# First product of the experts for the last 1,024 tokens: seven products of half blocks in place of eight

## Chip, cores and metric

One core of one Trainium2 chip. The time is the device time of one execution in microseconds (us); the kernel before has a median of 1032.53 us over 3 runs (1032.23 to 1032.94). TensorE is PE in the profile (PEld is its weight load), VectorE DVE, ScalarE ACT, GpSimd POOL; SP issues the DMAs.

## What is computed

Causal attention with a decay (4 batches, 8 heads, 576 tokens, head size 64), and on its output a mixture of 4 experts with two products each:

```python
attn_out = _attn_ref(**attn_kwargs)
x = attn_out.transpose(0, 2, 1, 3).reshape(B * S, H * D)   # 2304 x 512
p = domain_probs / (domain_probs.sum(-1, keepdims=True) + 1e-09)
for e in range(E):                                          # E = 4
    h = np.maximum(x @ w1[e], 0.0)                          # w1[e]: 512 x 1024
    out += p[:, e:e + 1] * (h @ w2[e])                      # w2[e]: 1024 x 512
```

All is in float32. TensorE is fed with float32r, so each product is made of three: a value is split into a high part (rounded to float32r) and a low part (the rest), and high x high, high x low and low x high are added in PSUM.

## The kernel before

**Tokens** are in 9 chunks of 256 (`CH`), numbered in the order in which the attention finishes them. **Hidden units** are in 32 blocks of 128, eight for each expert. A weight tile `wr` is 128 x 1024 (512 KB): its left half is w1 for one block (four slices of 128 columns, one for each quarter of the 512 inputs), its right half w2 for that block. `w_load` (line 579) issues its DMA on SP into one of 2 buffers, `w_split` (line 584) makes the high part `wh` on ACT and the low part `wl` with two subtractions of 512 columns on POOL (on DVE for the even ones of the first 16 tiles). `wh` and `wl` have 6 buffers each.

**A step** (class `Step`, line 604) is one chunk with two hidden blocks. `l1` (line 610) makes the hidden values: 2 blocks x 4 slices x 3 = 24 matmuls, 256 columns each, into a PSUM tile of `ps_1`. `gate` (line 628) applies the relu and splits: ACT writes `gh`, DVE writes `gl`. `l2` (line 641) is the second product: 2 halves of the chunk x 2 blocks x 3 = 12 matmuls of 512 columns into two tiles of `ps_2`, which two steps (`ps` 0 and 1) fill together. `gather` (line 660) then adds the tile, times the expert's probability, to the chunk's accumulator `acc` on DVE, and after the last one issues the output DMA.

**The order** is `SWEEPS` (line 24): sweep 0 has 28 steps with chunks 0 to 2, sweep 1 has 52 with chunks 1 to 4, sweep 2 has 64 with chunks 5 to 8 (each of 16 pairs of weight tiles meets the four chunks one after another). The main loop (line 797) writes `l1` of step n, then `l2` of step n - 1, and `w_split` for tiles 6 further on when a pair has met its last chunk. Instructions run on each engine in an order that a planner sets while the program is built: by the order written, but an instruction that is not ready in the planner's own model of time lets later ones go ahead.

**The attention** is cut into small pieces (`head_steps`, line 540), each with a cost: for a head of the second half of the tokens three pieces of scores (2072 in all), three of transposes (1500) and one of the product with v (600), so 4172. `pace` (line 727) writes these pieces between the steps, so that the summed cost follows a broken line through goals: a chunk must be done `LEAD` = 3 steps ahead of its first use. The pieces of the 24 heads that follow the startup in the first half and the 32 heads of the second half add up to 169,120. Its last instruction is `fin` (line 490), which writes the attention's output: for chunks 0 to 4 split into `xh` and `xl`, for chunks 5 to 8 as float32 into `xf`, and `widen` (line 527) splits these when the chunk is first used (ACT `xh`, DVE `xl`, 1024 columns each).

Of the kernel before, what the change touches and what calls it, by code (L numbers as in the profile page):

```python
# [8 lines left out]
F32 = mybir.dt.float32  # L9
# [8 lines left out]
CH = 256  # L18
# [5 lines left out]
SWEEPS = (  # L24
    ((0,), (0,), (0, 1), (0, 1, 2)),
    ((1, 2, 3, 4), (1, 2, 3, 4), (2, 3, 4), (3, 4)),
    ((5, 6, 7, 8), (5, 6, 7, 8), (5, 6, 7, 8), (5, 6, 7, 8)),
)
DIRECT = (0, 1, 2, 3, 4)
LEAD = 3  # L30
W_DVE = tuple(range(0, 16, 2))
W_SLOT = (4, 6)
NEAR = 2
JOBS = ((0, 0), (1, 0), (2, 0), (3, 0), (0, 1), (1, 1), (2, 1), (3, 1))
# [34 lines left out]
def fused(ctx: ExitStack, tc: tile.TileContext, qk, v, f, probs, w, out):  # L69
# [3 lines left out]
        tc.tile_pool(name=name, bufs=bufs, space=bass.MemoryType.PSUM)  # L73
    )
    const = SB("const", 1)
    raw_p = SB("raw", 1)
    hi_p = SB("hi", 2)
    p_p = SB("p", 6)
    pt_p = SB("pt", 1)
    v_p = SB("v", 2)  # L80
    x_p = SB("x", 2)
    st_p = SB("st", 4)
    xh_p = SB("xh", 4)
    xf_p = SB("xf", 4)
    w_p = SB("w", 6)
    wr_p = SB("wr", 2)
    g_p = SB("g", 2)
    acc_p = SB("acc", 4)
    dr_p = ctx.enter_context(tc.tile_pool(name="dr", bufs=4, space=bass.MemoryType.DRAM))
    ps_a = PS("ps_a", 4)  # L90
    ps_1 = PS("ps_1", 2)
# [432 lines left out]
                            op=ALU.mult,  # L524
                        )

    def widen(c):
        th, tl = x_tiles(c)
        nc.scalar.activation(out=th, in_=xf[c], func=AF.Copy)
        nc.vector.tensor_tensor(out=tl, in0=xf[c], in1=th.bitcast(F32), op=ALU.subtract)  # L530


    jobs = []
    for b, half in JOBS:
# [39 lines left out]


    wh, wl, wraw = {}, {}, {}
    NW = len(SWEEPS) * E * (FF // 128)

    def w_load(n):
        if n < NW and n not in wraw:  # L580
# [1 line left out]
            nc.sync.dma_start(out=wraw[n], in_=w[n % 32])  # L582

    def w_split(n):
        if n >= NW:
            return
        w_load(n)
        wh[n] = w_p.tile([128, 1024], F32R, tag="wh", name=f"wh{n}")
        wl[n] = w_p.tile([128, 1024], F32R, tag="wl", name=f"wl{n}")
        r = wraw.pop(n)  # L590
        nc.scalar.activation(out=wh[n], in_=r, func=AF.Copy)  # L591
        for a in (0, 512):
            z = a + 512
            eng = nc.vector if n in W_DVE else nc.gpsimd
            eng.tensor_tensor(  # L595
                out=wl[n][:, a:z], in0=r[:, a:z], in1=wh[n][:, a:z].bitcast(F32), op=ALU.subtract
            )
        w_load(n + 1)
        w_load(n + 2)

    acc = {}
    l2 = {}

    class Step:
# [36 lines left out]
        def l2(self, q):  # L641
            tt, fi = divmod(q, 2)
            if self.ps == 0 and fi == 0:
                l2[tt] = ps_2.tile([128, DM], F32, tag="l2", name=f"l2_{self.nm}_{tt}")
            n = self.w0 + fi
            a = self.gh[:, fi, tt * 128 : (tt + 1) * 128]
            z = self.gl[:, fi, tt * 128 : (tt + 1) * 128]
            x, y = wh[n][:, 512:], wl[n][:, 512:]
            for m, (lhsT, rhs) in enumerate(((a, x), (a, y), (z, x))):
                nc.tensor.matmul(  # L650
                    out=l2[tt],
                    lhsT=lhsT,
                    rhs=rhs,
                    start=(self.ps == 0 and fi == 0 and m == 0),
                    stop=(self.ps == 1 and fi == 1 and m == 2),
                )
            if self.ps == 1 and fi == 1:
                self.gather(tt)

        def gather(self, tt):  # L660
            c, e = self.c, self.g // 2
            if tt == 0:
                seen[c] += 1
            if c not in acc:
                acc[c] = acc_p.tile([128, 2, DM], F32, tag="acc", name=f"acc{c}")
            sc = prob[:, 2 * c + tt, e : e + 1]
            if seen[c] == 1:
                nc.vector.tensor_scalar(
                    out=acc[c][:, tt, :], in0=l2[tt], scalar1=sc, scalar2=None, op0=ALU.mult
                )  # L670
            else:
                nc.vector.scalar_tensor_tensor(  # L672
                    out=acc[c][:, tt, :],
                    in0=l2[tt],
                    scalar=sc,
                    in1=acc[c][:, tt, :],
                    op0=ALU.mult,
                    op1=ALU.add,
                )
            if seen[c] == 2 * E:  # L680
                for o, r0, n in rows_of(c, tt):
                    nc.sync.dma_start(out=out[r0 : r0 + n, :], in_=acc[c][o : o + n, tt, :])

    seen = {c: 0 for c in range(NCH)}
    steps = [
# [9 lines left out]
    for n in range(len(heads) + 1):  # L695
        if n >= FIRST:
            asteps.extend(head_steps(n))
        stage_end.append(len(asteps))
    cost = [0.0]
    for c, _ in asteps:  # L700
        cost.append(cost[-1] + c)
# [16 lines left out]
        first.setdefault(t.c, n)  # L718
    marks = [(0, cost[need[steps[0].c]])]
    goals = sorted((max(n - LEAD, 1), cost[need[c]]) for c, n in first.items() if n > 0)  # L720
    while goals:
        n0, c0 = marks[-1]
        best = max(goals, key=lambda m: ((m[1] - c0) / (m[0] - n0), m[0]))
# [73 lines left out]
    for n in range(len(steps) + 1):  # L797
        cur = steps[n] if n < len(steps) else None
        if cur is not None:
            if cur.c not in used:  # L800
                used.add(cur.c)
                upto(need[cur.c])
                if cur.c not in DIRECT:
                    widen(cur.c)
            for q in range(4):
                cur.l1(q)
                pace(n + q / 8)
            cur.gate()
        if prev is not None:
            for q in range(4):  # L810
                prev.l2(q)
                pace(n + (q + 4) / 8)
            if prev.c == SWEEPS[prev.s][prev.g // 2][-1]:
                base = prev.w0 + 6
                w_split(base)
                w_split(base + 1)
        prev = cur


# [41 lines left out]
```

## Time and profile before

| | |
|---|---|
| time of the profiled execution | 1032.68 us |
| its span, first to last instruction | 1031.0 us |
| median of 3 runs | 1032.53 us |
| PE busy | 1004.5 us, 97% |
| DVE, ACT, POOL busy | 541.7, 451.9, 320.3 us |
| mean granted TensorE clock | 0.988 of full speed |

Matmuls are pipelined: the record of one matmul (mean 285 ns for 256 columns) is longer than the distance to the next. What a matmul costs in a dense stretch is therefore read from the chain of work that ended last, which counts the matmuls of a stretch and its length. In the chain and in the timeline a line begins with its start and its duration in us; a bracket at the end of a timeline line tells how long the engine had been idle before and who released it. In a list of groups, "x144 | 99.3, 690 |" means 144 instructions, 99.3 us in all, 690 ns each, and behind the next bar is the idle time before them.

### The profile page before, as it was taken

How to read it: one execution, taken by the hardware profiler on the slowest of the kernel's cores; microseconds unless marked ns; L12 is line 12 of the kernel's file. 1: busy time of each engine (PE TensorE's matmuls, PEld its weight loads, DVE VectorE, ACT ScalarE, POOL GpSimd, SP SyncE). 2: the span in 40 equal slices, each digit the busy share in tenths (PEclk: the TensorE clock that was granted, in tenths of full speed). 3: DMA queues.
4: the chain of work that ended last, by engine and by line, in shares of the span. 5: the costliest groups of instructions: out<-in, count | busy, mean ns of one | idle time of the engine just before them, and what ended most of it. 6: DMA issues, size and time to landing. Idle time of an engine off the chain costs nothing.

```text
span 1031.0 us, 16823 instructions
## 1 busy us (share of the span) xinstructions
PE 1004.5 (97%) x6544; PEld 917.3 (89%) x6544; DVE 541.7 (53%) x1184; ACT 451.9 (44%) x909; POOL 320.3 (31%) x346
## 2 busy tenths in 40 slices
PE   4799999999999999999999999999999999999998
PEld 4697899989999999999999999999999999999997
DVE  6767766586877856677466665532222222222222
ACT  6766666566656535445455455422121211212110
POOL 4756876341403204031223144213030311303010
PEclk9599999999999999999999999999999999999999
DMA  5445544252412214032131331211120202112001
GB/s 179 134 148 166 164 133 130 74 165 85 131 50 90 90 50 131 15 93 95 62 118 54 111 118 62 90 54 47 37 82 1 83 21 62 51 32 82 1 22 62
DMA packets 30447, 87.02 MB, mean 84 GB/s; under 512 B 3268, under 2 KB 5376, under 8 KB 30368
## 3 DMA queue, kind: packets, MB, share of 16 engines
q1 hardware_dynamic: 30368, 85.94, 26.4%
q8 instruction: 52, 0.85, 0.3%
q14 instruction: 27, 0.22, 0.1%
HBM read 81.06 MB, written 4.87 MB: 83 GB/s over the span
## 4 chain that ended last, share of the span: by engine, by line
PE 89%; DMA 4%; DVE 3%; ACT 2%; issue 1%; POOL 1%; SPq 1%; ACTq 0%; POOLq 0%; DVEq 0%
PE l L620 38%; PE l L650 36%; PE s L314 5%; PE t L406 5%; PE o L456 4%; DMA wr<-in_w 2%; DVE v L249 1%; PE b L374 1%; DMA raw<-in_qk 1%; ACT wh L591 1%; DMA pr_r<-in_probs 1%; POOL wl L595 0%; DVE xl L506 0%; DVE p L328 0%; DVE wl L595 0%
## 5 line engine op out<-in xcount | busy, mean ns | idle before, releaser
L595 POOL TENSOR_TENSOR wl<-wr,wh 128x512 fp32r<-128x512 f32 x176 | 228.1, 1325 | 351.3 <-ACT wh L591 345.5
L620 PE MATMUL l<-xh,wh 128*128 128x256 f32 x1152 | 330.9, 288 | 1.2 <-ACT xh L503 1.0
L620 PE MATMUL l<-xl,wh 128*128 128x256 f32 x1152 | 328.8, 285 | 0.1
L620 PE MATMUL l<-xh,wl 128*128 128x256 f32 x1152 | 328.2, 285 | 0.0
L632 DVE SCALAR_TENSOR_TENSOR gl<-l,gh 128x512 fp32r<-128x512 f32 x144 | 99.3, 690 | 276.3 <-ACT gh L631 275.5
L650 PE MATMUL l<-wh,gh 128*128 128x512 f32 x576 | 230.5, 400 | 0.4 <-DVE rs L362 0.4
L650 PE MATMUL l<-wl,gh 128*128 128x512 f32 x576 | 227.8, 395 | 0.0
L620 PEld LDWEIGHTS l<-xh,wh 128*128 128x128 f32 x1152 | 220.9, 192 | 6.5 <-ACT xh L503 1.6
L620 PEld LDWEIGHTS l<-xl,wh 128*128 128x128 f32 x1152 | 221.3, 192 | 5.8 <-DVE xl L506 0.5
L650 PE MATMUL l<-wh,gl 128*128 128x512 f32 x576 | 225.8, 393 | 0.0
L620 PEld LDWEIGHTS l<-xh,wl 128*128 128x128 f32 x1152 | 221.3, 192 | 0.7 <-DVE wl L595 0.2
L631 ACT ACTIVATE gh<-l 128x512 fp32r<-128x512 f32 x144 | 85.6, 594 | 277.7 <-PE l L620 276.9
L343 ACT ACTIVATE p<-p,nm 128x576 f32<-128x576 f32 (+2 forms) x160 | 96.1, 601 | 97.3 <-DVE nm L328 96.7
L591 ACT ACTIVATE wh<-wr 128x1024 fp32r<-128x1024 f32 x96 | 99.9, 1054 | 69.3 <-DMA wr<-in_w 39.9
L650 PEld LDWEIGHTS l<-wh,gl 128*128 128x128 f32 x576 | 108.3, 188 | 22.6
L650 PEld LDWEIGHTS l<-wh,gh 128*128 128x128 f32 x576 | 108.8, 189 | 16.8 <-issue 0.6
L650 PEld LDWEIGHTS l<-wl,gh 128*128 128x128 f32 x576 | 109.0, 189 | 14.9
L672 DVE SCALAR_TENSOR_TENSOR acc<-l,prob,acc 128x512 f32<-128x512 f32 x126 | 94.0, 748 | 26.8 <-PE l L650 24.0
L328 DVE CUSTOM_DVE_ANT_0 p<-s,mask 128x288 f32<-128x288 f32 (+2 forms) x160 | 75.6, 477 | 49.4 <-PE s L314 48.4
L262 POOL CAST q<-raw 64x320 fp32r<-64x320 f32 (+1 forms) x56 | 27.1, 484 | 235.7 <-PE s L314 210.9
L423 DVE TENSOR_TENSOR ptl<-t,pth 128x320 fp32r<-128x320 f32 (+2 forms) x120 | 66.1, 553 | 60.9 <-ACT pth L416 60.4
L406 PE MATMUL t<-ident,p 128*128 128x128 f32 x480 | 83.7, 283 | 5.6 <-ACT p L343 3.5
(73 smaller groups left out, 1003.2 us busy)
## 6 DMA issues: line engine op xcount, KB each, us to landing
wr<-in_w SPq DMA_DIRECT2D x96, 512.0 KB
raw<-in_qk SPq DMA_DIRECT2D x16, 896.0 KB
raw<-in_qk SPq DMA_DIRECT2D x12, 512.0 KB
vr<-in_v SPq DMA_DIRECT2D x16, 320.0 KB
out<-acc SPq DMA_DIRECT2D x16, 256.0 KB
first<-in_qk SPq DMA_DIRECT2D x4, 512.0 KB
vr<-in_v SPq DMA_DIRECT2D x12, 128.0 KB
first<-in_v SPq DMA_DIRECT2D x1, 512.0 KB
```

The lines of the kernel that those rows point to most:

```text
L314: nc.tensor.matmul(out=ps[:, at : at + z - a], lhsT=lhsT, rhs=rhs, start=(m == 0), stop=(m == 1),)
L328: nc.vector.tensor_tensor_reduce(out=pt[:, a:z], in0=ps, in1=mask[:, m0 + a : m0 + z], scale=-0.125, scalar=BIG if n == 0 else nm[:, col : ...
L343: nc.scalar.activation(out=pt[:, :w_], in_=pt[:, :w_], func=AF.Exp, scale=-1.0, bias=self.nmax[hh][:, c : c + 1], accum_out=self.ssum[:, h ...
L406: nc.tensor.transpose(ps[:, at : at + 128], self.p[hh, it][:, TOK0[jt] : TOK0[jt] + 128], ident)
L423: nc.vector.tensor_tensor(out=lo[:, a0 + first : a0 + at - first], in0=ps[:, 2 * first : at], in1=hi[:, a0 + first : a0 + at - first].bitc ...
L591: nc.scalar.activation(out=wh[n], in_=r, func=AF.Copy)
L595: eng.tensor_tensor(out=wl[n][:, a:z], in0=r[:, a:z], in1=wh[n][:, a:z].bitcast(F32), op=ALU.subtract)
L620: nc.tensor.matmul(out=self.l1p[:, fi, :], lhsT=lhsT, rhs=rhs[:, k, :], start=(k == 0 and m == 0), stop=(k == 3 and m == 2),)
L631: nc.scalar.activation(out=self.gh, in_=self.l1p, func=AF.Relu)
L632: nc.vector.scalar_tensor_tensor(out=self.gl, in0=self.l1p, scalar=0.0, in1=self.gh.bitcast(F32), op0=ALU.max, op1=ALU.subtract,)
L650: nc.tensor.matmul(out=l2[tt], lhsT=lhsT, rhs=rhs, start=(self.ps == 0 and fi == 0 and m == 0), stop=(self.ps == 1 and fi == 1 and m == 2),)
L672: nc.vector.scalar_tensor_tensor(out=acc[c][:, tt, :], in0=l2[tt], scalar=sc, in1=acc[c][:, tt, :], op0=ALU.mult, op1=ALU.add,)
```

## The change

Sweep 2 goes. In its place come 16 pairs `Big(p)`, each one pair of weight tiles (256 hidden units) with all 1,024 tokens of chunks 5 to 8. The first product is seen as 2 x 2 blocks (hidden blocks of 128, inputs in halves of 256, tokens in halves of 512: chunks 5, 6 and chunks 7, 8) and made with seven products in place of eight (Strassen's scheme in Winograd's form): four sums of weight blocks (`SUMS`) and four of token blocks (`XSUMS`), seven products of 2 slices x 3 = 6 matmuls with 512 columns (`PRODUCTS`), and seven sums of the results (`Big.l1`). `x_piece` makes and splits the seven token blocks once, in two parts each; `big_split` makes and splits the weight blocks of a pair into three `wh` and `wl` tiles (the four sums; the three unsummed blocks; w2). The blocks of x lie in a pool that is opened in the memory of the attention's pools once those are closed (`open_late`); the split hidden values lie where `xh` and `xl` were. `gather` is called for each pair (16 times a chunk half) in place of each second step (8 times). `wr` gets a third buffer. The attention's pieces, with 14 of `x_piece` behind them (costs 200 and 300, 3,600 in all), have as last goal step 76 of the 80 steps that are left. A line of "..." marks what is left out.

```diff
 SWEEPS = (
     ((0,), (0,), (0, 1), (0, 1, 2)),
     ((1, 2, 3, 4), (1, 2, 3, 4), (2, 3, 4), (3, 4)),
-    ((5, 6, 7, 8), (5, 6, 7, 8), (5, 6, 7, 8), (5, 6, 7, 8)),
 )
 DIRECT = (0, 1, 2, 3, 4)
 LEAD = 3
 W_DVE = tuple(range(0, 16, 2))
+LAST = (5, 6, 7, 8)
+AHEAD = 4
...
     st_p = SB("st", 4)
-    xh_p = SB("xh", 4)
     xf_p = SB("xf", 4)
     w_p = SB("w", 6)
-    wr_p = SB("wr", 2)
+    wr_p = SB("wr", 3)
     g_p = SB("g", 2)
     acc_p = SB("acc", 4)
+    early = ExitStack()
+    chunks = ExitStack()
+    AT = lambda name, bufs: early.enter_context(tc.tile_pool(name=name, bufs=bufs))
+    raw_p = AT("raw", 1)
+    hi_p = AT("hi", 2)
+    p_p = AT("p", 6)
+    pt_p = AT("pt", 1)
+    v_p = AT("v", 2)
+    x_p = AT("x", 2)
+    xh_p = chunks.enter_context(tc.tile_pool(name="xh", bufs=4, side="right"))
...
-    def widen(c):
-        th, tl = x_tiles(c)
-        nc.scalar.activation(out=th, in_=xf[c], func=AF.Copy)
-        nc.vector.tensor_tensor(out=tl, in0=xf[c], in1=th.bitcast(F32), op=ALU.subtract)
-
...
     wh, wl, wraw = {}, {}, {}
-    NW = len(SWEEPS) * E * (FF // 128)
+    NW = 3 * E * (FF // 128)
+    NS = len(SWEEPS) * E * (FF // 128)
...
     def w_split(n):
-        if n >= NW:
+        if n >= NS:
+            if n % 2 == 0:
+                big_split((n - NS) // 2)
             return
...
         w_load(n + 1)
         w_load(n + 2)
+        w_load(n + 3)
...
                 )
             if self.ps == 1 and fi == 1:
-                self.gather(tt)
...
+                gather(self.c, tt, self.g // 2, l2[tt], 2 * E)
+    def gather(c, tt, e, ps, times):
...
+        if seen[c] == times:
+            for o, r0, n in rows_of(c, tt):
+                nc.sync.dma_start(out=out[r0 : r0 + n, :], in_=acc[c][o : o + n, tt, :])
...
+    SUMS = (
+        (1, (1, 0), (1, 1), ALU.add),
+        (2, 1, (0, 0), ALU.subtract),
+        (3, (0, 0), (1, 0), ALU.subtract),
+        (4, (0, 1), 2, ALU.subtract),
+    )
+    XSUMS = (
+        (1, (0, 1), (0, 0), ALU.subtract),
+        (2, (1, 1), 1, ALU.subtract),
+        (4, 2, (1, 0), ALU.subtract),
+        (3, (1, 1), (0, 1), ALU.subtract),
+    )
+    PRODUCTS = {
+        1: (1, 256, (0, 0)),
+        2: (1, 512, (1, 0)),
+        3: (0, 768, (1, 1)),
+        4: (1, 0, 4),
+        5: (0, 0, 1),
+        6: (0, 256, 2),
+        7: (0, 512, 3),
+    }
+    late = ExitStack()
+    rh, rl, bw, xs_ = {}, {}, {}, {}
+    def open_late():
+        early.close()
+        late.x = late.enter_context(tc.tile_pool(name="rx", bufs=1))
+    def x_piece(i, k, op=None, *of):
+        if k not in rh:
+            rh[k] = late.x.tile([128, 2, 512], F32R, tag=f"rh{k}", name=f"rh_{len(rh)}")
+            rl[k] = late.x.tile([128, 2, 512], F32R, tag=f"rl{k}", name=f"rl_{len(rl)}")
+        hi, lo = (t[:, :, CH * i : CH * (i + 1)] for t in (rh[k], rl[k]))
+        x_of = lambda b: (
+            xf[LAST[2 * b[1] + i]][:, 2 * b[0] : 2 * b[0] + 2, :]
+            if type(b) is tuple
+            else xs_[b, i]
+        )
+        if op is None:
+            x = x_of(k)
+        else:
+            x = xs_[k, i] = late.x.tile([128, 2, CH], F32, tag="t", name=f"rx{k}_{i}", bufs=2)
+            nc.gpsimd.tensor_tensor(out=x, in0=x_of(of[0]), in1=x_of(of[1]), op=op)
+        nc.scalar.activation(out=hi, in_=x, func=AF.Copy)
+        nc.vector.tensor_tensor(out=lo, in0=x, in1=hi.bitcast(F32), op=ALU.subtract)
+    def big_split(p):
+        if p >= 16:
+            return
+        n = NS + 2 * p
+        w_load(n)
+        w_load(n + 1)
+        r = [wraw.pop(n), wraw.pop(n + 1)]
+        part = lambda b: r[b[0]][:, 256 * b[1] : 256 * b[1] + 256]
+        t = late.x.tile([128, 4, 256], F32, tag="wt", name=f"wt{p}", bufs=1)
+        w_of = lambda b: part(b) if type(b) is tuple else t[:, b - 1, :]
+        for k, a, z, op in SUMS:
+            nc.gpsimd.tensor_tensor(out=t[:, k - 1, :], in0=w_of(a), in1=w_of(z), op=op)
+        tiles = []
+        for k in range(3):
+            tiles.append(
+                [
+                    w_p.tile([128, 1024], F32R, tag=x, name=f"b{x}{p}_{k}") for x in ("wh", "wl")
+                ]
+            )
+        f = t.rearrange("p k n -> p (k n)")
+        jobs_ = [
+            (0, 0, f),
+            (1, 0, part((1, 1))),
+            (1, 256, part((0, 0))),
+            (1, 512, part((0, 1))),
+            (2, 0, r[0][:, 512:]),
+            (2, 512, r[1][:, 512:]),
+        ]
+        for k, c, x in jobs_:
+            w_ = x.shape[1]
+            hi, lo = (y[:, c : c + w_] for y in tiles[k])
+            nc.scalar.activation(out=hi, in_=x, func=AF.Copy)
+            for a in range(0, w_, 512):
+                z = min(a + 512, w_)
+                nc.gpsimd.tensor_tensor(
+                    out=lo[:, a:z], in0=x[:, a:z], in1=hi[:, a:z].bitcast(F32), op=ALU.subtract
                 )
+        bw[p] = tiles
+        for k in range(2, 5):
+            w_load(n + k)
+    class Big:
+        def __init__(self, p):
+            self.p, self.e = p, p // 4
+        def product(self, m):
+            ps = ps_a.tile([128, 512], F32, tag="a", name=f"m{self.p}_{m}")
+            k0, c, b = PRODUCTS[m]
+            a, z = (t[:, c : c + 256] for t in bw[self.p][k0])
+            for k in range(2):
+                o = slice(128 * k, 128 * k + 128)
+                for i, (lhsT, rhs) in enumerate(((a, rh[b]), (a, rl[b]), (z, rh[b]))):
+                    nc.tensor.matmul(
+                        out=ps,
+                        lhsT=lhsT[:, o],
+                        rhs=rhs[:, k, :],
+                        start=(k == 0 and i == 0),
+                        stop=(k == 1 and i == 2),
+                    )
+            return ps
+        def add(self, tag, ps, x, op=ALU.add, out=None, flip=False):
+            if out is None:
+                out = g_p.tile([128, 512], F32, tag=tag, name=f"u{self.p}_{len(self.u)}")
+                self.u.append(out)
+            if x is None:
+                nc.scalar.activation(out=out, in_=ps, func=AF.Copy)
             else:
+                a, z = (x, ps) if flip else (ps, x)
+                nc.vector.tensor_tensor(out=out, in0=a, in1=z, op=op)
+            return out
+        def gate(self, b, x):
+            hi, lo = (
+                late.h.tile([128, 512], F32R, tag=t, name=f"{t}{self.p}_{b[0]}{b[1]}")
+                for t in ("hh", "hl")
+            )
+            nc.scalar.activation(out=hi, in_=x, func=AF.Relu)
+            nc.vector.scalar_tensor_tensor(
+                out=lo, in0=x, scalar=0.0, in1=hi.bitcast(F32), op0=ALU.max, op1=ALU.subtract
+            )
+            self.h[b] = hi, lo
+        def l1(self):
+            self.h, self.u = {}, []
+            e1 = self.add("gh", self.product(1), None)
+            u2 = self.add("gl", self.product(6), e1)
+            self.add(None, self.product(2), e1, out=e1)
+            self.gate((0, 0), e1)
+            p5 = self.product(5)
+            u4 = self.add("gh", p5, u2)
+            self.add(None, self.product(7), u2, out=u2)
+            c22 = self.add("gl", p5, u2)
+            self.gate((1, 1), c22)
+            self.add(None, self.product(3), u4, out=u4)
+            self.gate((0, 1), u4)
+            self.add(None, self.product(4), u2, ALU.subtract, out=u2, flip=True)
+            self.gate((1, 0), u2)
+        def l2(self, q):
+            for u in (2 * q, 2 * q + 1):
+                half, o = divmod(128 * u, 512)
+                pool, tag = ((ps_2, "l2"), (ps_1, "l1"))[u % 2]
+                ps = pool.tile([128, DM], F32, tag=tag, name=f"y{self.p}_{u}")
+                for fi in range(2):
+                    a, z = (t[:, o : o + 128] for t in self.h[fi, half])
+                    x, y = (t[:, 512 * fi : 512 * fi + 512] for t in bw[self.p][2])
+                    for m, (lhsT, rhs) in enumerate(((a, x), (a, y), (z, x))):
+                        nc.tensor.matmul(
+                            out=ps,
+                            lhsT=lhsT,
+                            rhs=rhs,
+                            start=(fi == 0 and m == 0),
+                            stop=(fi == 1 and m == 2),
+                        )
+                gather(LAST[u // 2], u % 2, self.e, ps, 16)
...
         stage_end.append(len(asteps))
+    asteps.append((0, open_late))
+    for i in range(2):
+        for k in ((0, 0), (1, 0), (1, 1)):
+            asteps.append((200, lambda k=k, i=i: x_piece(i, k)))
+        for k, a_, z_, op in XSUMS:
+            asteps.append((300, lambda k=k, i=i, a_=a_, z_=z_, op=op: x_piece(i, k, op, a_, z_)))
     cost = [0.0]
...
     goals = sorted((max(n - LEAD, 1), cost[need[c]]) for c, n in first.items() if n > 0)
+    goals.append((len(steps) - AHEAD, cost[-1]))
     while goals:
...
                 upto(need[cur.c])
-                if cur.c not in DIRECT:
-                    widen(cur.c)
             for q in range(4):
                 cur.l1(q)
                 pace(n + q / 8)
             cur.gate()
+        else:
+            upto(len(asteps))
+            chunks.close()
+            late.h = late.enter_context(tc.tile_pool(name="h", bufs=8, side="right"))
+            big = [Big(p) for p in range(16)]
+            big[0].l1()
         if prev is not None:
             for q in range(4):
...
+    for p in range(16):
+        if p + 1 < 16:
+            big[p + 1].l1()
+        for q in range(4):
+            big[p].l2(q)
+        big_split(p + 3)
+    late.close()
```

## Rows read from the trace of the kernel before

**Rows 1.** The page, engines: busy time, share of the span and instructions.

```profile
PE 1004.5 (97%) x6544; PEld 917.3 (89%) x6544; DVE 541.7 (53%) x1184; ACT 451.9 (44%) x909; POOL 320.3 (31%) x346
```

**Rows 2.** The page, chain that ended last: shares of the span by engine.

```profile
PE 89%; DMA 4%; DVE 3%; ACT 2%; issue 1%; POOL 1%; SPq 1%; ACTq 0%; POOLq 0%; DVEq 0%
```

**Rows 3.** Stretches: us of busy time (instructions) of PE, PEld, DVE, ACT, POOL, clock, DMA, GB/s.

```profile
200.00:300.00 100.00, 99.33 (x674) 91.73 (x673) 77.70 (x180) 63.61 (x131) 29.13 (x33) 1.00 0.33 106
500.00:600.00 100.00, 100.00 (x668) 91.95 (x667) 63.66 (x143) 51.12 (x98) 26.64 (x26) 1.00 0.27 89
700.00:1027.00 327.00, 327.00 (x2086) 297.73 (x2085) 84.37 (x117) 61.34 (x84) 65.74 (x52) 1.00 0.14 44
```

**Rows 4.** The chain in order of time, end of the kernel.

```profile
1013.04 2.87 PE l L620 x24
1015.91 2.75 PE l L650 x12
1018.66 2.87 PE l L620 x24
1021.53 5.48 PE l L650 x24
1027.02 0.02 issue
1027.04 0.75 DVE acc L672
```

**Rows 5.** The chain in order of time, where sweep 2 begins.

```profile
660.56 0.70 PE l L620 x6
...
668.71 0.72 PE l L620 x6
...
675.84 2.87 PE l L620 x24
```

**Rows 6.** Timeline of DVE: the attention's last two writes to `xf`.

```profile
674.52 0.54 DVE L520 TENSOR_TENSOR xf<-xs,b 128x64 f32<-128x64 f32 x2
```

**Rows 7.** Groups of POOL by shape.

```profile
L595 POOL TENSOR_TENSOR wl<-wr,wh 128x512 fp32r<-128x512 f32 x176 | 228.1, 1325 | 351.3 <-ACT wh L591 345.5 <-issue 5.6
L270 POOL TENSOR_TENSOR kl<-raw,hi 64x256 fp32r<-64x256 f32 x24 | 18.4, 767 | 6.4 <-ACT hi L261 6.4
```

**Rows 8.** Groups of ACT by shape.

```profile
L591 ACT ACTIVATE wh<-wr 128x1024 fp32r<-128x1024 f32 x96 | 99.9, 1054 | 69.3 <-DMA wr<-in_w 39.9 <-PE l L650 21.5 <-PE s L314 3.9
L631 ACT ACTIVATE gh<-l 128x512 fp32r<-128x512 f32 x144 | 85.6, 594 | 277.7 <-PE l L620 276.9
L503 ACT ACTIVATE xh<-xs 128x256 fp32r<-128x256 f32 x20 | 8.3, 413 | 17.4 <-DVE xs L497 17.3
```

**Rows 9.** Groups of DVE by shape.

```profile
L632 DVE SCALAR_TENSOR_TENSOR gl<-l,gh 128x512 fp32r<-128x512 f32 x144 | 99.3, 690 | 276.3 <-ACT gh L631 275.5
L672 DVE SCALAR_TENSOR_TENSOR acc<-l,prob,acc 128x512 f32<-128x512 f32 x126 | 94.0, 748 | 26.8 <-PE l L650 24.0
L423 DVE TENSOR_TENSOR ptl<-t,pth 128x512 fp32r<-128x512 f32 x32 | 21.9, 686 | 19.8 <-ACT pth L416 19.7
L530 DVE TENSOR_TENSOR xl<-xf,xh 128x1024 fp32r<-128x1024 f32 x4 | 6.4, 1613 | 0.8 <-ACT xh L529 0.8
```

**Rows 10.** All instructions on the tile `wr`: duration in ns, least, median, most.

```profile
L595 POOL TENSOR_TENSOR wl<-wr,wh x176: 1272/1296/2269, 35.0 to 983.6; 128x512 fp32r<-128x512 f32 x176
L595 DVE TENSOR_TENSOR wl<-wr,wh x16: 677/689/1325, 26.4 to 92.4; 128x512 fp32r<-128x512 f32 x16
```

**Rows 11.** Timelines of SP and of ACT in sweep 2: a weight tile's load and its split.

```profile
757.65 2.82 SPq L582 DMA_DIRECT2D wr<-in_w  x2
...
761.41 1.06 ACT L591 ACTIVATE wh<-wr 128x1024 fp32r<-128x1024 f32 x1 [3.38 <-DMA wr<-in_w]
```

**Rows 12.** Waits of PE and of SP: us in total, times, longest.

```profile
PE s L314 <- DVE hi L276: 8.9, 1, 8.9
PE t L406 <- ACT p L343: 3.5, 5, 1.6
...
SPq L582 <- POOL wl L595: 139.4, 64, 3.1
```

**Rows 13.** Timeline of SP, end of the kernel: the last output DMAs.

```profile
1026.91 1.25 SPq L682 DMA_DIRECT2D out<-acc  x2
```

More of the change, by code (lines that the diff above doesn't have):

```diff
@@ L75, in fused @@
     const = SB("const", 1)
[L76 to L81, printed above, removed]
     st_p = SB("st", 4)
-    xh_p = SB("xh", 4)
     xf_p = SB("xf", 4)
     w_p = SB("w", 6)
-    wr_p = SB("wr", 2)
+    wr_p = SB("wr", 3)
     g_p = SB("g", 2)
     acc_p = SB("acc", 4)
+    early = ExitStack()
[8 more added lines that the diff above has]
+    xh_p = chunks.enter_context(tc.tile_pool(name="xh", bufs=4, side="right"))
     dr_p = ctx.enter_context(tc.tile_pool(name="dr", bufs=4, space=bass.MemoryType.DRAM))
@@ L657, in l2 @@
             if self.ps == 1 and fi == 1:
-                self.gather(tt)
[L660 to L669, printed above, removed]
-                )
-            else:
[L672 to L682, printed above, removed]
+                gather(self.c, tt, self.g // 2, l2[tt], 2 * E)
@@ new lines, in gather @@
+    def gather(c, tt, e, ps, times):
+        if tt == 0:
+            seen[c] += 1
+        if c not in acc:
+            acc[c] = acc_p.tile([128, 2, DM], F32, tag="acc", name=f"acc{c}")
+        sc = prob[:, 2 * c + tt, e : e + 1]
+        if seen[c] == 1:
+            nc.vector.tensor_scalar(
+                out=acc[c][:, tt, :], in0=ps, scalar1=sc, scalar2=None, op0=ALU.mult
+            )
+        else:
+            nc.vector.scalar_tensor_tensor(
+                out=acc[c][:, tt, :],
+                in0=ps,
+                scalar=sc,
+                in1=acc[c][:, tt, :],
+                op0=ALU.mult,
+                op1=ALU.add,
+            )
+        if seen[c] == times:
+            for o, r0, n in rows_of(c, tt):
+                nc.sync.dma_start(out=out[r0 : r0 + n, :], in_=acc[c][o : o + n, tt, :])
@@ new lines, in fused @@
+    class Big:
[22 more added lines that the diff above has]
+                nc.scalar.activation(out=out, in_=ps, func=AF.Copy)
+            else:
+                a, z = (x, ps) if flip else (ps, x)
[7 more added lines that the diff above has]
+            nc.scalar.activation(out=hi, in_=x, func=AF.Relu)
+            nc.vector.scalar_tensor_tensor(
+                out=lo, in0=x, scalar=0.0, in1=hi.bitcast(F32), op0=ALU.max, op1=ALU.subtract
+            )
+            self.h[b] = hi, lo
[29 more added lines that the diff above has]
+                            stop=(fi == 1 and m == 2),
+                        )
+                gather(LAST[u // 2], u % 2, self.e, ps, 16)
@@ L808, in fused @@
             cur.gate()
+        else:
+            upto(len(asteps))
[3 more added lines that the diff above has]
+            big[0].l1()
         if prev is not None:
```

## Prediction

> **What bounds it now.** I read the page's table of engines first: PE is busy for 97% of the span, the next engine for 53% [rows 1]. Busy time of PE is no proof, since its records overlap, so the chain of work that ended last comes second: 89% of it lies on PE, 3% on DVE and 2% on ACT [rows 2]. Then the stretches: from 700 us to the end of the matmuls PE has no pause in the records, while DVE is busy for 84 of 327 us, ACT for 61 and POOL for 66 [rows 3]. There the kernel is TensorE and little else; the other three could take three times their work. With the attention beside it (200 to 600 us) DVE stands at 64 to 78%, and PE still at 99 to 100 [rows 3]. The waits agree: the longest of PE on another engine is one of 8.9 us, the next kinds sum to 3.5 us and less [rows 12]. So a matmul that goes from sweep 2 is time that goes, as long as the rest keeps up.
>
> **What the seven products save.** In the chain, 24 matmuls of `l1` (256 columns) take 2.87 us, 0.1196 us each; 12 of `l2` (512 columns) take 2.75 us, 0.229 each [rows 4]. A step is 5.62 us. Removed: 64 steps x 2.87 = 183.7 us. Added: 16 pairs x 7 products x 6 = 672 matmuls of 512 columns. No row has this product, but the same form with other operands is `l2`: 672 x 0.229 = 153.9 us. The second product keeps its 64 x 12 matmuls. Saved: **29.8 us**, 1.86 us for a pair; a pair then takes 42 x 0.229 = 9.6 us of `l1` and 48 x 0.229 = 11.0 us of `l2`, 20.6 us.
>
> Only a part of that is the eighth product. By columns, 1536 x 256 less 672 x 512 is 49,152, and at the full clock that the stretch was granted (1.00 [rows 3], the level of 2.4 GHz) this is 20.5 us. The rest comes from the wider matmul: two of 256 columns cost 0.239 us, one of 512 costs 0.229. The Trainium skill (TensorE: Matmul & The Clock Gate, Back-to-back issue gap) gives a gap of columns / 2.4 plus 2.5 ns, 109 and 216 ns, at which the sum would be about 22.7 us, an estimate. The trace is above that rule at both widths, and the measurement decides.
>
> **Work added beside the matmuls, for a pair of 20.6 us.**
> - POOL: 4 sums and 3 low parts of 256 columns, 4 low parts of 512. The nearest row for 256 is the subtraction of 64x256, 0.767 us; 512 take 1.325 [rows 7]. 7 x 0.767 + 4 x 1.325 = 10.7 us, 52%, where two splits now cost 5.3.
> - ACT: one copy out of PSUM and four relus at 0.594, copies of 1024 (1.054), 3 x 256 (0.413) and 2 x 512 (0.594): 3.0 + 3.5 = 6.5 us [rows 8].
> - DVE: 7 sums with one PSUM operand (nearest the `ptl` subtraction, 0.686), 4 gates at 0.69, 8 gathers at 0.748: 13.6 us, 66% [rows 9]. The gates now read two SBUF operands. The subtraction of that kind on DVE took 0.689 at the median and 1.325 at most, on POOL 1.296 and 2.269 [rows 10]. So between nothing and 4 x 0.64 = 2.5 us more on DVE, 16.1 at most; I take nothing.
> All three hide below 20.6 us of PE. If that cover were gone, DVE would be the first to show.
>
> **PSUM.** The products use the four banks of `ps_a`, which the attention no longer needs. A bank is wanted again four products later, so there are 3 x 1.37 = 4.1 us from a product's end to the reuse. The longest need is product 5, read by two sums that wait for product 7, and its bank is wanted only by the next `l1`, 11 us on. DVE has 7.6 us of work in the 9.6 us of `l1`. I cost this at nothing.
>
> **Weights in the steady state.** A pair now holds its two raw tiles until w2 is split. Its chain: a load of 512 KB lands and is first read 3.8 us after the SP issue [rows 11], sums 3.1 us, copy 1.05, low parts 2.65 and 2.3, w2 2.65: 15.6 us, below 20.6. Three `wh` tiles for each pair in 6 buffers: the last tile of pair p + 1 finds a buffer when `l1` of pair p has ended, 31 us ahead of `l1` of pair p + 2. Slack, so nothing; the bound is in the rivals. The third buffer's `w_load` waits on SP ahead of the attention's loads and output DMAs; such waits now are 3.1 us at most [rows 12], and those loads are issued two heads ahead, so I cost it at nothing.
>
> **The hand-over.** This has no row and is where the change can lose. Let T be the start of `l1` of pair 0. All attention matmuls lie ahead of it as before, so T itself doesn't move by them. The last attention pieces: before, 169,120 units end at step 81, which began at 668.7 us [rows 5]; the last write to `xf` ended at 675.1 [rows 6], so it lags 6 to 7 us. Pace: the 98,056 units from step 31 to 81 were 1961 a step; now 101,656 until step 76 are 2259 a step, and the attention proper ends at step 74.4. The first 31 steps already run at 2267, and DVE at 78% there left PE 99.3 [rows 3], so the denser pace costs nothing or a few us; I take nothing. Step 74.4 lies 5.6 steps ahead of T, about 32 us; minus the lag, the output is whole 25 us ahead of T. Then 14 pieces: POOL 8 x 1.325 = 10.6 us, ACT 14 x 0.594 = 8.3, DVE 14 x 0.81 (half the `widen` row) = 11.3 [rows 7 to 9]. They run beside one another, some 13 us, hidden if nothing else is in the queue. But POOL also has the splits of the last two tiles of sweep 1 (5.3 us) and pair 0's two first tiles (8.1 us): 24 us in 25. Pair 1 is worse: the load of its second raw tile waits until pair 0's w2 is split, which waits for a buffer that comes free at T. T + 2 (first w2 half) + 3.8 (load) + 3.1 + 1.05 + 2.65 + 1.5 = T + 14, where `l1` of pair 1 could begin at T + 9.6 + 2.75 = T + 12.4. So 1.6 us of stall there, at the least 0 (PE may be given `l2` of pair 0 first) and, with POOL late by the attention's lag once more, some 8. I take **2.5 us**.
>
> **The end.** The last gather began when the last matmul had issued, and the last output DMA went out about a us later, as now [rows 4, 13]. Eight output tiles of 256 KB now come in 11.0 us, 191 GB/s; the stretches shown reached 106 GB/s at a DMA share of 0.33 [rows 3]. Nothing to 1 us; I take nothing.
>
> **Sum.** The profiled execution took 1032.68 us, 0.15 above the median of 1032.53. 1032.7 - 29.8 + 2.5 = **1005.4 us**.
>
> **Rivals.**
> - *Only the eighth is saved.* If a matmul of 512 columns in the new product cost twice one of 256 (0.239 us), the saving would be an eighth of 183.7, 23.0 us: 1012.2. For it: the new product streams x, not w2. Against: `l2` has just this form and costs 0.229 [rows 4]. Chance 0.07. The rule of the Trainium skill named above (same page and section) would put the time near this one, by its own gaps; the trace speaks against it.
> - *A long hand-over.* The pool of the new x blocks lies in the attention's memory. If none of it can be written until the attention's last instruction, and that comes 10 us later than I reckon, POOL's 24 us ahead of `l1` run out in the open: 10 to 20 us of PE idle, 1013 to 1023. For it: POOL is nearly full there by the sum above. Against: PE reaches a given step later too when the attention is late. Chance 0.13.
> - *DVE bounds the pair.* If each gate pays the worst row (2.5 us) and the chain of sums cannot be spread over `l2`, 1 us shows in each pair: 1021. Against: 16.1 us of 20.6. Chance 0.03.
> - *Slower: the weights bound the pair.* If the raw tiles are held until w2 gets the buffer that the same pair's predecessor frees at the end of its `l2`, load, sums and splits (15.6 us) cannot overlap with that `l2`; a pair then takes 11 + 15.6 = 26.6 us, 16 x 6 = 96 us more than forecast, some 1100. It decides from a pair of 22.5 us (5.62 x 4), 1.9 us above forecast. For it: 6 buffers are two pairs, and three are in flight. Against: two of a pair's three tiles come free after its `l1`. Chance 0.04.
> - *The change does not do what it says*: the products cannot be fewer than written, as the order is fixed while building; no chance of its own.
>
> **Chances and range.** The forecast's own range is 1002 (no stall) to 1011 (8 us), chance 0.73. Up to 1016 it takes in the first rival and the shorter half of the second: 0.73 + 0.07 + 0.05, less the edges. Below 1001.5 nothing in the sum reaches. A measurement can tell 0.2%, 2.1 us. Faster: the forecast, the first two rivals and most of the third, 0.95; same 0.01; slower 0.04.
>
> **What would show it.** Right: 672 matmuls of 512 columns at some 0.229 us in the chain, a pair each 20.6 us, PE without pauses but at the hand-over; POOL near 52% and DVE near 66% from some 670 us on. Wrong: waits of the new matmuls on POOL's or ACT's weight parts in each pair (the slower rival), on DVE's sums (the third), or one long pause near 665 us behind x pieces (the second). If the granted clock falls there, the second is dearer: the page shows a pause of that kind nowhere.

## The result and the profile after

The changed kernel takes 999.65 us (median of 4 runs, 998.15 to 1000.12), before 1032.38 on the same chip: ratio 0.968 with a 95% interval of 0.966 to 0.970. That is 32.7 us less, where 27.1 were forecast; the range's lower end was 1001.5, 1.9 us above the result. The direction and most of the sum came out, but the change did more than the prediction read out of it. The page after, engines and chain [rows 1, 2]:

```profile
PE 973.3 (97%) x5680; PEld 857.3 (86%) x5680; DVE 675.0 (68%) x1370; ACT 483.3 (48%) x999; POOL 418.0 (42%) x466
...
PE 89%; DVE 3%; POOL 3%; DMA 2%; ACT 2%; issue 1%; SPq 0%; ACTq 0%; POOLq 0%
```

PE has 864 matmuls less (6544 to 5680: 1536 out, 672 in) and is as full as before. In the steady stretch of the pairs (columns as in [rows 3]) PE has no pause, DVE is busy for 65% (66 forecast), POOL for 51% (52 forecast):

```profile
690.00:960.00 270.00, 270.00 (x1171) 219.75 (x1170) 176.17 (x250) 82.53 (x144) 137.75 (x147) 1.00 0.16 49
```

**The hand-over** ended nearly when it was forecast. In the lines from here on `m` is the PSUM tile of one of the seven products and `y` that of the second product; `wt` are the sums of weight blocks, `bwh` and `bwl` the high and low parts of a pair's weights, `rx` the sums of token blocks, `rh` and `rl` their high and low parts; SPq is the queue in which SP issues DMAs. Timelines of DVE, PE, SP and POOL in the changed kernel, in order of time:

```profile
630.66 0.55 DVE L525 TENSOR_TENSOR xf<-xs,b 128x64 f32<-128x64 f32 x2
...
658.17 0.39 PE L794 MATMUL m<-rh,bwh 128*128 128x512 f32 x1
...
662.95 1.59 SPq L583 DMA_DIRECT2D wr<-in_w  x2
...
666.54 0.74 POOL L751 TENSOR_TENSOR wt<-wr 128x256 f32<-128x256 f32 x1 [2.37 <-DMA wr<-in_w]
...
671.25 0.50 PE L794 MATMUL m<-rh,bwh 128*128 128x512 f32 x1 [0.69 <-ACT bwh L771]
```

The attention's output is whole at 631.2 us, 27 us ahead of the first product (25 forecast). Pair 1's second raw tile is asked for 4.8 us after that product (2 forecast), lands 3.5 us later, and its first weight part lets PE go on 13.1 us after T, the start of that product (14 forecast). Up to then PE had run the 42 matmuls of pair 0's products and 12 of `l2`, as the prediction had it, and it waited 0.69 us in place of 1.6. The good agreement is in part luck, since two errors met: the load was asked for 2.8 us later than forecast, and the low parts, 4.15 us of the forecast, held nothing up, since pair 1's first products began with matmuls on the high parts. Those 0.7 us are all that PE waited for pair 1's weights; 2.5 had been taken. The 14 low parts of the x pieces took 0.96 to 1.06 us each on DVE in the mean, not 0.81, and that did no harm.

Up to the pairs the changed kernel had gained some 6 us. Its first product starts at 658.2 us, where step 80 of before started at 660.4. And before still had 33 attention matmuls to run behind that start, about 3.9 us of the chain, the last of them at 672.6 us; in the changed kernel the last one ran at 629.4 us.

**Where the rest came from.** The chain in order of time, end of the kernel and a stretch ahead of the pairs:

```profile
608.36 1.41 PE l L624 x12
...
970.48 2.75 PE m L794 x12
973.23 21.24 PE y L852 x91
994.47 0.02 issue
994.50 0.75 DVE acc L676
```

Three distances differ from what the sum used. `l1` of the first two sweeps, which the change does not touch, runs at 1.41 / 12 = 117.5 ns where it was 119.6 [rows 4]. The new first product runs at 227 to 229 ns as forecast. But the second product, whose form did not change, is slower: 21.24 / 91 = 233.4 ns, against 228.3 (5.48 / 24) [rows 4].

And early on, the chain of before from 56 to 125 us lay on weight loads for 29%; after it does not. The heads of the two answers (shares by line), before and after:

```profile
by line: DMA wr<-in_w 29.3%; PE l L620 12.1%; DVE v L249 11.6%; issue 10.5%; PE l L650 9.4%; POOL wl L595 5.5%; ACT wh L591 4.7%; DVE xl L506 2.6%; ACT tmp L470 2.2%; PE t L406 1.6%; DVE xs L497 1.2%; PE o L456 1.2%; DVE gl L632 1.0%; DVE p
```

```profile
by line: PE l L654 40.3%; PE l L624 39.8%; PE o L461 6.5%; PE s L319 6.4%; PE t L411 5.5%; PE b L379 1.6%
```

Pieces of that chain before:

```profile
72.18 4.33 DMA wr<-in_w
76.59 0.13 ACT wh L591
76.72 0.96 issue
77.67 0.39 ACT tmp L470
78.12 0.42 issue
78.54 1.99 DVE v L249 x2
80.54 0.33 SPq L220
...
81.00 3.91 DMA wr<-in_w
84.99 1.07 ACT wh L591
```

With two raw buffers a load could be asked for only when a split had freed one; ACT stood at the next split until it landed, and behind that in ACT's queue stood an attention copy (`tmp`) that later work needed. Here that work is DVE's on `v`, for which a load on SP waited (line 220), and the next weight load stood in SP's queue behind that one. PE shows the loss: between 80 and 100 us it was busy for 17.55 us before and for all 20 after (columns as in [rows 3], before, then after).

```profile
80.00:100.00 20.00, 17.55 (x114) 14.69 (x112) 14.94 (x35) 12.73 (x29) 10.96 (x15) 1.00 0.58 169
80.00:100.00 20.00, 20.00 (x141) 18.46 (x140) 16.37 (x41) 15.99 (x36) 14.36 (x17) 1.00 0.63 197
```

The change gives `wr` a third buffer.

### The profile page after: what moved, and what is told of

The parts are those of the page before. It is cut to its first block, busy times and chain, and to the rows that moved or that the text cites. A ratio compares the mean times of both kernels' runs of the same rounds, so it can differ in the third digit from the quotient of the medians.

```text
span 998.3 us, 15506 instructions
## 1 busy us (share of the span) xinstructions
PE 973.3 (97%) x5680; PEld 857.3 (86%) x5680; DVE 675.0 (68%) x1370; ACT 483.3 (48%) x999; POOL 418.0 (42%) x466
## 4 chain that ended last, share of the span: by engine, by line
PE 89%; DVE 3%; POOL 3%; DMA 2%; ACT 2%; issue 1%; SPq 0%; ACTq 0%; POOLq 0%
PE l L624 21%; PE l L654 20%; PE y L852 18%; PE m L794 14%; PE s L319 6%; PE t L411 5%; PE o L461 5%; PE b L379 1%; POOL bwl L774 1%; DVE rl L738 1%; DMA raw<-in_qk 1%; POOL rx L736 1%; POOL wl L598 1%; POOL wt L751 1%; ACT wh L594 0%
## 5 line engine op out<-in xcount | busy, mean ns | idle before, releaser
L624 PE MATMUL l<-xh,wh 128*128 128x256 f32 x640 | 185.6, 291 | 0.7 <-ACT xh L508 0.5
L624 PE MATMUL l<-xh,wl 128*128 128x256 f32 x640 | 183.1, 286 | 0.0
L624 PE MATMUL l<-xl,wh 128*128 128x256 f32 x640 | 182.9, 286 | 0.0
L654 PE MATMUL l<-wh,gh 128*128 128x512 f32 x320 | 129.6, 405 | 0.4 <-ACT gh L635 0.4
L654 PE MATMUL l<-wl,gh 128*128 128x512 f32 x320 | 127.1, 397 | 0.0
L654 PE MATMUL l<-wh,gl 128*128 128x512 f32 x320 | 126.7, 398 | 0.0
L624 PEld LDWEIGHTS l<-xh,wh 128*128 128x128 f32 x640 | 122.1, 191 | 3.8 <-ACT xh L508 1.1
L852 PE MATMUL y<-bwl,hh 128*128 128x512 f32 x256 | 101.2, 396 | 0.0
L852 PE MATMUL y<-bwh,hh 128*128 128x512 f32 x256 | 101.2, 395 | 0.0
L852 PE MATMUL y<-bwh,hl 128*128 128x512 f32 x256 | 100.9, 396 | 0.0
```

Of the source, the lines that this page charges most:

```text
L624: nc.tensor.matmul(out=self.l1p[:, fi, :], lhsT=lhsT, rhs=rhs[:, k, :], start=(k == 0 and m == 0), stop=(k == 3 and m == 2),)
L654: nc.tensor.matmul(out=l2[tt], lhsT=lhsT, rhs=rhs, start=(self.ps == 0 and fi == 0 and m == 0), stop=(self.ps == 1 and fi == 1 and m == 2),)
L852: nc.tensor.matmul(out=ps, lhsT=lhsT, rhs=rhs, start=(fi == 0 and m == 0), stop=(fi == 1 and m == 2),)
```

## The experiments

The kernels ran in three groups, each beside the kernel before on one chip; its medians there were 1031.76, 1032.04 and 1032.16 us, and kernels of different groups are compared by their ratios to it. Two theories for the extra gain ahead of the pairs came first: A, the third buffer; B, the attention's denser pace or another order by the planner.

**b_third.** The kernel before with the third buffer alone.

```diff
-    wr_p = SB("wr", 2)
+    wr_p = SB("wr", 3)
...
         w_load(n + 2)
+        w_load(n + 3)
```

> The kernel before with a third raw weight buffer and one more load ahead, nothing else. Theory A (the third buffer gave the 5 to 7 us that the change won ahead of the last sweep, by taking the weight loads off ACT's queue): 1025 to 1027.5 us, the pause of PE near 80 to 100 us gone. Theory B (the denser pace of the attention, or another order by the planner, gave them): within 1 us of 1032.4.

1028.42 us, ratio 0.9964 (0.9952 to 0.9977): 3.7 us less by the ratio. The loads left the early chain (same answer, 56 to 125 us):

```profile
by line: PE l L651 38.9%; PE l L621 35.9%; PE o L456 5.8%; PE s L314 5.5%; PE t L406 4.9%; DVE v L249 3.9%; PE b L374 1.6%; ACT wh L591 1.5%; issue 0.9%; DVE xs L497 0.6%; ACT tmp L470 0.6%; DVE xs L478 0.1%
```

ACT's idle time ahead of `wh` that ended with a load falls from 39.9 us [rows 8] to 5.3, between 56 and 150 us from 9.8 to 1.0, and PE is busy for 20.0 us between 80 and 100 us. The granted clock is not the cause: the runs of before beside it that were granted a mean of 0.999 or more of full speed (2.4 GHz) took 1030.86 to 1032.68 us, the five of `b_third` (0.998 or more) 1026.38 to 1029.34. With the buffer the planner also sets another order (PE has another instruction than before at 554 of its 6544 places), so the 3.7 us belong to the buffer together with the order that follows from it. The buffer is a cause, but at 3.7 us, below the 5 to 7 of theory A, too small for the whole.

**b_pace.** The kernel before with the denser pace alone.

```diff
+    goals.append((76, cost[-1]))
+    goals.sort()
```

> The kernel before with the attention's last goal at step 76, as in the changed one, nothing else. Theory A: within 1.5 us of 1032.4, since the pace only moves work between engines that wait. Theory B: 1025 to 1028.

1032.33 us, ratio 1.0006 (0.9997 to 1.0015): no difference. The pace falls out of theory B.

**a_two.** The changed kernel with two raw buffers.

```diff
-    wr_p = SB("wr", 3)
+    wr_p = SB("wr", 2)
...
-        w_load(n + 3)
...
-        for k in range(2, 5):
+        for k in range(2, 4):
             w_load(n + k)
```

> The changed kernel with two raw buffers and one load ahead less. Theory A: the 5 to 7 us are lost again, and a pair whose two raw tiles fill both buffers waits for its loads: load 3.8, sums 3.1, copy 1.05, low parts 7.6 us, 15.6 of 20.6, so no more is lost in the steady state: 1004 to 1008 us. Theory B: 999 to 1001. If the pairs turn out to be bound by their weights: over 1030.

1007.59 us, ratio 0.9767 (0.9753 to 0.978): by the ratios 8.9 us of the gain gone, more than the 3.7 of `b_third`. At the hand-over the chain now runs through loads, and PE waits 3.1 us on POOL's and 1.1 on ACT's weight parts (chain from 655 to 720 us, then waits of PE):

```profile
658.47 8.04 POOL bwl L773 x7
666.52 5.26 DMA wr<-in_w
...
712.13 7.25 POOL bwl L773 x6
719.39 5.00 DMA wr<-in_w
```

```profile
PE m L793 <- POOL bwl L773: 3.1, 2, 1.9
...
PE m L793 <- ACT bwh L770: 1.1, 1, 1.1
```

The pairs are not bound by their weights even so, as the second half of the expectation had it: from 720 to 1000 us PE is busy for 278.9 of 280 us.

**a_eight.** Eight products of half blocks in place of seven, 512 columns wide; the sums of results are left out.

```diff
-            e1 = self.add("gh", self.product(1), None)
...
+            W = {(0, 0): (1, 256), (0, 1): (1, 512), (1, 0): (0, 768), (1, 1): (1, 0)}
...
+                    for kk in range(2):
+                        k0, c = W[fi, kk]
...
+                    self.gate((fi, half), ps)
```

> The changed kernel with eight products of 512 columns in place of seven (12 matmuls into each of four tiles; no sums of results; the weight sums and three of the four x sums are still made). 96 matmuls of 512 columns more at 0.2275 us: 21.8 us, so 1021 to 1022 us. Rival (only the eighth is saved by the change, width brings nothing, and the rest of the gain is elsewhere): 999.7 + 23 to 26 us and as much less in the stretch ahead. A rival by which DVE's sums slow the pairs: less than 21.8 us more, since 7 of 19 DVE instructions of a pair are gone.

1020.31 us, ratio 0.9886 (0.9873 to 0.99): 0.0205 above the changed kernel's ratio, 21 us. So the eighth product is worth 21 us, and DVE's sums, which are gone here, cost nothing beyond the two intervals (some 2 us). Its products stand in the chain at 9.76 / 43 = 227 ns.

```profile
960.06 9.76 PE m L841 x43
```

The buffer explains 3.7 of the some 6 us gained ahead of the pairs, the pace none, and neither says why `l1` takes 117.5 ns in place of 119.6 over 1920 matmuls, or why the second product got slower. Theory C: the place of `xh` and `xl`, which the change had moved to the other end of the on-chip memory so that their pool can be closed. In the build's addresses, `xh` starts at 960 within 1024 bytes before (a multiple of 64) and at 992 after (an odd multiple of 32); `hh` and `hl`, which take that place in the pairs, at 992 too.

**b_right** and **b_shift.** The kernel before with `xh` and `xl` at the other end; then left in place, but moved by 32 bytes. In both, every engine has the same work as before, in `b_right` instruction for instruction.

```diff
-    xh_p = SB("xh", 4)
+    xh_p = ctx.enter_context(tc.tile_pool(name="xh", bufs=4, side="right"))
```

```diff
+    SB("pad1", 1).tile([128, 8], F32, name="pad1")
     xh_p = SB("xh", 4)
+    SB("pad2", 1).tile([128, 8], F32, name="pad2")
```

> The kernel before with the pool of xh and xl at the other end of the on-chip memory, as in the changed one, nothing else; every engine has the same instructions in the same order. In the changed kernel a matmul of 256 columns of l1 takes 117 ns from start to start at the median, before 120. Theory C (the place of xh and xl does that): 3456 x 2.7 ns = 9 us less, 1022 to 1024 us, and 117 ns. Rival (the planner's order or the third buffer does): 1031 to 1033 us and 120 ns.

> The kernel before with xh and xl left where they are but moved by 32 bytes (start 992 in place of 960 within 1024 bytes), and all behind them by 64. Theory C1 (it is the start within a line of 64 bytes that sets a matmul's distance): 117 ns, 1022 to 1024 us, as with the pool at the other end. Theory C2 (it is the region of the memory): 120 ns, 1031 to 1033 us.

1025.72 us, ratio 0.9933 (0.992 to 0.9945), and 1028.92, ratio 0.997 (0.996 to 0.9981). The chain of `b_right` has 24 matmuls of `l1` in 2.80 us where they took 2.87 [rows 4]:

```profile
1006.16 2.80 PE l L620 x24
```

The place matters, though `b_right` gains 6.9 us where 9 were expected, and `b_shift` 3.1, between the ranges of both its theories: its median distance is 117 ns like in `b_right`, but the mean 118.2 against 116.8, and `l2` goes from 229.1 to 230.3 (start to start, after 720 us). `b_shift` is no clean test of 32 bytes, since it also moved the weights, `gh` and `gl` by 64. The next two kernels are one.

**a_align** and **a_hal.** The changed kernel with 32 bytes left free at that end, for all of the run (`xh` and `hh` both start at 960), and only behind the closing of `xh` (`xh` at 992, `hh` at 960).

```diff
+    ctx.enter_context(tc.tile_pool(name="pad", bufs=1, side="right")).tile([128, 8], F32, name="pad")
     xh_p = chunks.enter_context(tc.tile_pool(name="xh", bufs=4, side="right"))
```

```diff
             chunks.close()
+            late.enter_context(tc.tile_pool(name="pad", bufs=1, side="right")).tile(
+                [128, 8], F32, name="pad"
+            )
             late.h = late.enter_context(tc.tile_pool(name="h", bufs=8, side="right"))
```

> The changed kernel with 32 bytes left free at the end of the on-chip memory, so that xh, xl and the split hidden values hh and hl that take their place start at 960 within 1024 bytes in place of 992. Theory C1: l1 of the first two sweeps goes back to 120 ns (1920 x 2.7 ns = 5.2 us more), and the second product of the pairs, 232.5 ns now against 227 in l2, goes to 227 (768 x 5.5 ns = 4.2 us less): about 1 us more than the changed kernel in all, both shown by the distances. Theory C2: nothing moves, 117 and 232.5 ns, 999.7 us.

> The changed kernel with the 32 bytes left free only once xh and xl are closed: xh and xl start at 992 within 1024 bytes, hh and hl at 960. Theory C1: 117 ns for l1 and 227 for the second product of the pairs, 4.2 us less than the changed kernel: 995 to 996 us. Theory C2: 999.7 us, 117 and 232.5 ns.

996.22 us, ratio 0.9653 (0.9639 to 0.9667), and 993.46, ratio 0.9621 (0.9608 to 0.9635). The second product came down to 20.64 / 91 = 226.8 ns in `a_hal`, from 233.4:

```profile
965.79 20.64 PE y L852 x91
986.43 0.03 issue
986.46 0.75 DVE acc L676
```

768 x 6.6 ns is 5.1 us; by the ratios the gain is 6.2. The first product came down with it, from 228.1 to 226.7 ns in the mean after 720 us, another 0.9 us over its 672 matmuls. In `a_align` `l1` is back at 120 ns at the median (117 in the changed kernel and in `a_hal`), and of the 6.2 us 2.9 are left. So the place of `xh` is worth 3.3 us over the 1920 matmuls of `l1`, not the 5.2 expected, and `a_align` lies below the changed kernel, not 1 us above it. The mean fits that: from 150 to 620 us it is 119.1 ns in `a_align` and 117.4 in `a_hal` (distances below 160 ns), 1.7 apart. The same piece of the chain in `a_align`, then in `a_hal`:

```profile
614.26 2.15 PE l L625 x18
```

```profile
611.52 2.11 PE l L624 x18
```

`a_hal` beats both kernels.

**a_rx.** As `a_hal`, with the token blocks `rh` and `rl` moved by 32 bytes as well.

```diff
         early.close()
+        late.enter_context(tc.tile_pool(name="padx", bufs=1)).tile([128, 8], F32, name="padx")
```

> The changed kernel with hh and hl moved by 32 bytes, and the token blocks rh and rl, which stream through TensorE in the seven products, moved by 32 as well (start 736 in place of 704 within 1024 bytes). If a streamed operand that starts at an odd multiple of 32 bytes saves 2.7 ns for each matmul, whatever its width: m goes from 226.7 to 224 ns, 672 x 2.7 = 1.8 us less than 993.5. If it saves only in matmuls of 256 columns: 226.7 ns and 993.5 us.

997.92 us, ratio 0.9674 (0.9661 to 0.9688): slower than `a_hal`, not faster. The first product takes 5.60 / 24 = 233 ns, in `a_hal` 5.44 / 24 = 227. The chains of `a_rx` and of `a_hal`, same pieces:

```profile
713.62 5.60 PE m L795 x24
```

```profile
713.06 5.44 PE m L794 x24
```

My expectation of the sign was wrong: the start that makes `l1` (256 columns, `xh` streamed) faster makes the first product (512 columns, `rh` streamed) slower.

**b_both.** The kernel before with the third buffer and `xh` at the other end: the two edits of `b_third` and `b_right`, the riders of the change, which it carries beside its scheme.

> The kernel before with both riders of the change: the third raw weight buffer and the pool of xh and xl at the other end of the memory. Alone they gave 3.3 and 6.3 us. If they add up: 1022 to 1023 us, and the seven products themselves are worth this less the time of the changed kernel with hh and hl moved by 32 bytes (993.5 us): 28 to 30 us, as the prediction's sum had it. If both remove the same waits: 1025 to 1026 us, and the products are worth 32 us.

1021.14 us, ratio 0.9897 (0.9884 to 0.9911): 10.6 us less, where the two alone gave 3.7 and 6.9. They add up. Between this kernel and `a_hal`, which has the same two riders and no slow second product, lie 0.9897 - 0.9621 = 0.0276, **28.5 us**, uncertain by some 2 us by the intervals: the new scheme by itself, hand-over included, with `l1` at its faster 117 ns on both sides.

**a_ahead.** The changed kernel with everything due four steps earlier.

```diff
-AHEAD = 4
+AHEAD = 8
```

> The changed kernel with the attention and the x pieces due four steps earlier (step 72 of 80). If the hand-over still cost PE time (the prediction put 2.5 us on it; the trace shows gaps of 1 us or so near 671 and 676 us): 1 to 2 us less than 999.7. If those gaps are pair 1's weights, which wait for buffers and loads and not for the attention: 999.7, within 1 us. If the denser pace costs PE its cover: 1 to 5 us more.

1000.2 us, ratio 0.9692 (0.9679 to 0.9706): no difference from the changed kernel. Pair 1's wait is gone from PE, and one of 1.7 us on DVE's `gl` has taken its place (waits of PE, 620 to 700 us):

```profile
PE l L654 <- DVE gl L636: 1.7, 1, 1.7
PE l L654 <- ACT gh L635: 0.4, 1, 0.4
```

So earlier due dates alone win nothing at the hand-over.

## Why the prediction was right and where it was wrong

- *The seven products, 29.8 us.* Right. With the riders on both sides of the comparison the difference is 28.5 us, where the sum had 27.3 with its stall. The terms shifted a little against each other: `l1` at 117 ns makes the 1536 matmuls that go 4 us cheaper, and the 1440 that stay run at 227 ns in `a_hal`, not 229, 3 us cheaper too. The eighth product alone is 21 us (20.5 by columns), the wider matmul most of the rest (two of 256 columns at 116.8 ns against one of 512 at 226.7, 768 times: 5.3 us). The rival by which only an eighth of `l1`, 23.0 us, is saved falls: new products stand at 227 ns in the chain, not 239.
- *What the Trainium skill's gap (TensorE: Matmul & The Clock Gate, Back-to-back issue gap) would have given*, about 22.7 us by estimate, is below the 28.5 measured; the rows of before were the better guide. That section of the Trainium skill gives the formula for the gap of a single, isolated matmul, and for a stream of weight loads and matmuls about 131 ns at 512 columns. The streams here took 227 to 234 ns, nearer to the formula than to that figure.
- *Hand-over, 2.5 us.* The place (pair 1's weights, behind its raw tile) was right, and the size was 0.7 in the waits. That the time came out is in part luck: the load left 2.8 us late, and the low parts were not waited for.
- *Work beside the matmuls and PSUM, nothing.* Right: POOL and DVE came within a point of the forecast, and leaving out DVE's sums gained nothing in `a_eight`. The gates took 823 ns in the mean after 690 us, not 690, inside the bounds.
- *The third buffer, nothing.* **Wrong**, the first step that failed. I costed the extra `w_load` as a wait on SP and asked what stood behind it, but not what the buffer takes away: the waits for loads that stood in ACT's queue ([rows 8] shows 39.9 us of idle time ahead of `wh` that ended with a load; I used only that row's duration). Nor was 3.1 us the longest wait on SP, as I wrote from [rows 12]: that is the longest of one kind, and the same answer has the weight loads wait for ACT's `wh` for up to 35.3 us (`SPq L582 <- ACT wh L591: 267.1, 29, 35.3`). Before, the buffer is worth 3.7 us; in the changed kernel two buffers cost 8.9 us, of which 4.2 stand in PE's waits on weight parts.
- *"All attention matmuls lie ahead of it as before, so T itself doesn't move by them."* **Wrong**, the second step. The sum let nothing else move the work ahead of the pairs either: pools were moved, and I costed that at nothing without naming it. `xh` at its new place made `l1` faster (6.9 us over the 3456 matmuls of the kernel before in `b_right`, 3.3 over the 1920 that are left, `a_hal` against `a_align`), and `hh` there made the second product slower (6.2 us against `a_hal`). The sentence isn't right for the attention either: before, 33 of its matmuls ran behind the start of step 80. That changes no term, as they are in both kernels.
- *The account* by ratios: 10.6 us for the two riders, 28.5 for the scheme, less 6.2 for the place of `hh` and `hl`: 32.9, measured 32.7. The prediction had the middle term alone. This sum closes by construction, as each term is the difference between two kernels in a row. One that does not: 27.1 forecast, 3.7 for the buffer (`b_third`), 3.3 for `xh` (`a_hal` against `a_align`), 1.8 for the shorter hand-over, less 2.9 for the second product (768 matmuls at 232.9 ns in place of 229.1, means after 720 us) is 33.0.
- *The other rivals.* No pair is bound by its weights, even with two raw buffers (`a_two`, 1007.6 us, no 1100), nor by DVE; the long hand-over did not come, and earlier due dates ahead of it gained nothing (`a_ahead`).
- *The range.* Its lower end was the sum with no stall. It had no term for a gain ahead of the last sweep, where both riders work.

## What to carry to other kernels

A diff that is about one thing carries others: list every buffer count and every pool that moved, and ask of each what it takes away as well as what it adds. An engine that is half idle can still hold the bottleneck up, if it stands at a wait with work behind it that the bottleneck needs; the chain by stretch showed that here, the busy shares of the span did not. Where TensorE is the bound, read a matmul's distance for each operand pair, and look at the start addresses of its operands when two of the same form differ.

## What the runs showed of the hardware

The start of a matmul's operand in the on-chip memory changed the distance to the next matmul, with TensorE's instructions the same and in the same order. In three pairs of kernels only the start of one operand differs, by 32 bytes in its high and low part; "even" is a start at a multiple of 64 bytes, "odd" one 32 bytes further. For 512 columns, an odd stationary operand (`hh` and `hl`, the changed kernel against `a_hal`: 233.4 against 226.8 ns) and an odd streamed one (`rh` and `rl`, `a_rx` against `a_hal`: 233 against 227) both cost 6 ns, 3%. For 256 columns an odd streamed operand (`xh` and `xl`, `a_hal` against `a_align`) gained 3 ns at the median (117 against 120) and 1.7 in the mean.

Which unit counts is not shown: each even start was 64 bytes past a multiple of 128 and each odd one 96, and no others were tried in this way. `b_shift`, which also moved the weights and the gated values to multiples of 128, had other distances again. Why the sign turns between these products, whose widths and operands both differ, is open, and an odd stationary operand was not tried at 256 columns.
